# A layer-norm, linear-attention and ReLU-MLP block on one core: a new hand-written order, six normalisations moved to ScalarE, three transposes moved to DMA

## Chip, core, metric

The kernel runs on one core of one Trainium2 chip. The metric is the device time of one execution in microseconds. Lower is better.

## What is computed

The input `x` has 2048 rows of 512 bf16 values. The block is two residual branches, each behind a layer norm (mean and variance over the 512 columns, eps 1e-5, no weights):

```
ln  = layernorm(x);  q, k, v = split(ln @ wqkv)          # 32 heads of 16
phi(t) = (t + 1 if t > 0 else exp(t)) + 1e-6
kv  = sum_s phi(k)[s] (x) v[s] ;  z = sum_s phi(k)[s]    # per head
h   = x + ((phi(q) @ kv) / (phi(q) . z + 1e-6)) @ wo
out = h + relu(layernorm(h) @ w1) @ w2                   # w1: 512x1792, w2: 1792x512
```

## The kernel before

Rows are dealt to 16 tiles of 128 rows x 512 columns (`x_nat[:, t, :]`), and the tiles to four chunks of 512 rows for everything that works on transposed data (`lnT[c]`, `pqT[c]`). All of PSUM is one tensor `bk` of eight banks of 128 x 512 f32. Nothing is scheduled automatically: the string `ORDER` lists every step as a word such as `K.3.2`, and the loop at lines 548 to 550 calls `op_K(3, 2)`. The order of the words is the program order of each engine and of the DMA queue (all DMAs are issued by SyncE, one after the other), and the last number of most TensorE words is the PSUM bank. A step waits until its inputs are written and until the readers of what it overwrites are done; whatever stands behind it on the same engine waits too. So the order and the banks decide which engine idles.

The words that the change and the prediction's steps touch:

- `lx.t.n` loads n tiles of x (L201, SyncE); `lk`, `lq`, `lv`, `lo`, `l1`, `l2` load weights (L204).
- `warm.n.b`: n matmuls on zeros (L215); `const`, `masks`: small constants; `masks` is 3 memsets and 12 affine_selects on GpSimd (L181 to L193), read by `zh` and `kx`.
- First norm of tile t: `S.t`, `A.t` statistics on VectorE (L226, L227); `R.t.n` two ScalarE activations that make rstd for n tiles (L232, L233); `N.t` the normalisation itself, one VectorE tensor_scalar x - mean, times rstd, into `ln_nat` (L251).
- Transposes of a normalised tile into `lnT`: either `T.t.b`, four TensorE transposes into a bank (L270), followed by `E.t` (ScalarE, L280) or `V.t` (VectorE, L283), which copy the bank to `lnT`; or `X.t`, one DMA transpose issued by SyncE (L291). Before, tiles 0 to 6 go by T, tiles 7 to 15 by X.
- Keys: `K.t.b` four matmuls (L299); phi by `F` (exp, ScalarE, L317), `U` (relu, ScalarE, L320), `M` (min and add, VectorE, L324), `D` (add, VectorE, L327); `W` (L332) replaces U and D by one VectorE step that reads the bank. `Q.c.j.b` (L307) and `qF`, `qU`, `qM`, `qD`, `qW` are the same for queries.
- `G.t`: four matmuls that add a tile's phi(k) times `ln_nat` into banks 4 to 7 (L351); `za`, `zf`, `z`, `zc`, `zh`: the sum z.
- `gD`, `kv`, `kx` (L400), `m`, `mA` (ScalarE) or `mD` (VectorE): kv per head, masked and multiplied by wo.
- Denominators of chunk c: `dn` (L448), `dnl` and `dnx` (ScalarE, L454, L461), `dt.t` (DMA transposes, L480), `dm` (VectorE, L484). Then `h.t.b` (L494), `hD` (residual, L500), second norm `s`, `a`, `r`, `n`, transposed by `x.t` (DMA, L292) or `t.t.b` with `e` or `v`.
- MLP: `p.c.f.b` (L510), `pA` or `pD` (relu on ScalarE L516 or VectorE L521), `f` (L530), `fo` (VectorE, L538), `fd` (store, L545).

TensorE's own sequence is thus written out word by word: first the warm-up matmuls, then transposes, K and G mixed, Q, the kv product, h mixed with the first p, and p and f alternating to the end.

Of the kernel before, what the change touches and what calls it, by code (L numbers as in the profile page):

```python
# [580 lines left out]
```

## Time and profile before

| | us |
|---|---|
| median of 3 runs | 169.91 (169.8 to 170.13) |
| profiled execution, first to last instruction (span) | 168.6 |
| around the span, by the median | 1.3 |
| TensorE busy | 163.1 |
| VectorE busy | 104.7 |
| ScalarE busy | 64.3 |
| GpSimd busy | 4.8 |

A busy share is an average over stages. Matmuls are pipelined: each is shown with 379 ns though the next starts earlier, so the shown busy time hides small gaps, and gaps are found from the starts of successive groups. By stage the trace gives this (columns: window, its length, then busy us and instruction count for TensorE, its weight loads, VectorE, ScalarE, GpSimd; granted clock; DMA share; GB/s):

```profile
0.00:8.00 8.00, 5.61 (x25) 2.23 (x26) 5.27 (x19) 4.16 (x11) 4.80 (x21) 1.00 0.68 207
8.00:14.00 6.00, 5.83 (x36) 2.78 (x36) 5.62 (x17) 5.20 (x13) 0.00 (x0) 1.00 0.59 204
14.00:28.00 14.00, 14.00 (x69) 6.37 (x68) 14.00 (x37) 10.75 (x20) 0.00 (x0) 1.00 0.56 111
28.00:38.00 10.00, 10.00 (x62) 4.78 (x61) 9.53 (x16) 7.85 (x9) 0.00 (x0) 1.00 0.98 318
38.00:62.00 24.00, 23.84 (x166) 11.40 (x165) 19.80 (x39) 16.60 (x21) 0.00 (x0) 1.00 0.50 122
```

### The profile page before, as it was taken

To read this page: it belongs to the slowest core of one execution; us is meant where nothing else is said; L and a number is where in the kernel's file an instruction comes from. 1 tells how busy PE (TensorE), PEld (TensorE's weight loads), DVE (VectorE), ACT (ScalarE), POOL (GpSimd) and SP (SyncE) were. 2 spreads that over 40 slices of the span, in tenths; PEclk is the share of its full clock that TensorE was granted. 3 is DMA by queue.
4 is the path that set the end of the run, shared out by engine and by line. 5 is a ranking of instruction groups with operands and counts; after the bars stand their busy time and mean duration, and the time that the engine had idled before them with its cause. 6 is when DMAs were issued, how large, how long until landed. Compare 5 with 4: busy or idle time off the path is not lost.

```text
span 168.6 us, 2307 instructions
## 1 busy us (share of the span) xinstructions
PE 163.1 (97%) x875; PEld 76.3 (45%) x875; DVE 104.7 (62%) x207; ACT 64.3 (38%) x97; POOL 4.8 (3%) x21
## 2 busy tenths in 40 slices
...
DVE  3999999996879896978799725220066401007132
ACT  3699867775589755600201140170000203021000
POOL 7400000000000000000000000000000000000000
PEclk9999999999999999999999999999999999999999
...
GB/s 130 295 254 47 146 79 176 312 365 230 95 31 93 156 97 79 45 74 50 41 83 40 62 90 100 91 4 0 0 0 31 93 4 0 0 0 0 79 111 62
DMA packets 30091, 15.36 MB, mean 91 GB/s; under 512 B 22656, under 2 KB 29056, under 8 KB 30080
## 3 DMA queue, kind: packets, MB, share of 16 engines
...
q8 instruction: 7, 0.11, 0.3%
q14 instruction: 4, 0.03, 0.1%
HBM read 7.86 MB, written 2.10 MB: 59 GB/s over the span
## 4 chain that ended last, share of the span: by engine, by line
PE 84%; ACT 4%; DMA 4%; SPq 3%; DVE 2%; issue 1%; DVEq 0%; ACTq 0%
PE bk L530 29%; PE bk L510 29%; PE bk L351 7%; PE bk L299 7%; PE bk L494 6%; PE bk L307 5%; DMA wk_sb<-in_A_wqkv_dram 3%; ACT eb L317 1%; DMA rd<-wk_sb 1%; SPq L201 1%; SPq L480 1%; PE bk L448 1%; ACT rb L320 1%; DVE pqT L332 1%; ACT lnT L280 1%
## 5 line engine op out<-in xcount | busy, mean ns | idle before, releaser
L530 PE MATMUL bk<-w_sb,at 128*128 128x512 bf16 (+2 forms) x252 | 51.5, 355 | 0.0
L510 PE MATMUL bk<-lnT,w_sb 128*128 128x512 bf16 x224 | 51.4, 379 | 0.0
L516 ACT ACTIVATE at<-bk 128x1024 bf16<-128x1024 f32 x14 | 14.1, 1023 | 70.3 <-PE bk L510 70.3
L521 DVE TENSOR_SCALAR at<-bk 128x1024 bf16<-128x1024 f32 x14 | 17.0, 1221 | 33.7 <-PE bk L510 33.7
L530 PEld LDWEIGHTS <-at 128*128 128x128 bf16 x252 | 23.6, 98 | 25.2
L510 PEld LDWEIGHTS <-w_sb 128*128 128x128 bf16 x224 | 21.8, 98 | 26.0 <-issue 0.2
L538 DVE SCALAR_TENSOR_TENSOR gT<-bk,rstd,h_nat 128x512 bf16<-128x512 f32 (+2 forms) x18 | 12.0, 686 | 18.3 <-PE bk L530 15.9
L317 ACT ACTIVATE eb<-bk 128x1024 bf16<-128x1024 f32 (+1 forms) x18 | 16.5, 925 | 6.1 <-PE bk L299 3.5
L299 PE MATMUL bk<-wk_sb,lnT 128*128 128x512 bf16 x64 | 15.5, 379 | 0.6 <-DMA wk_sb<-in_A_wqkv_dram 0.5
L494 PE MATMUL bk<-m_sb,pqs 128*128 128x512 bf16 x64 | 15.5, 379 | 0.1
L307 PE MATMUL bk<-lnT,wq_sb 128*128 128x512 bf16 x64 | 15.1, 379 | 0.1
L320 ACT ACTIVATE rb<-bk 128x1024 bf16<-128x1024 f32 (+1 forms) x15 | 13.6, 906 | 1.2 <-PE bk L307 1.2
L351 PE MATMUL bk<-at,h_nat 128*128 128x512 bf16 x56 | 13.7, 379 | 0.0
L500 DVE TENSOR_TENSOR h_nat<-bk,x_nat 128x512 bf16<-128x512 f32 x16 | 10.8, 678 | 2.7 <-PE bk L494 2.6
L226 DVE BATCH_NORM_STATS2 st<-x_nat 128x6 f32<-128x512 bf16 x16 | 10.6, 678 | 1.8 <-DMA x_nat<-in_A_x_dram 1.8
L228 DVE BATCH_NORM_STATS2 st<-h_nat 128x6 f32<-128x512 bf16 x16 | 10.5, 679 | 0.0
L299 PEld LDWEIGHTS <-lnT 128*128 128x128 bf16 x64 | 5.9, 98 | 8.2 <-ACT lnT L280 1.2
L494 PEld LDWEIGHTS <-pqs 128*128 128x128 bf16 x64 | 6.1, 98 | 7.9 <-DVE pqs L484 1.2
L307 PEld LDWEIGHTS <-wq_sb 128*128 128x128 bf16 x64 | 6.1, 97 | 7.3 <-issue 0.4
L351 PEld LDWEIGHTS <-h_nat 128*128 128x128 bf16 x64 | 6.0, 98 | 6.6
L461 ACT ACTIVATE wk_sb<-ld 128x1024 bf16<-128x1024 f32 x8 | 8.0, 1048 | 0.1
L324 DVE TENSOR_SCALAR eb<-eb 128x1024 bf16<-128x1024 bf16 (+1 forms) x18 | 6.9, 388 | 1.2 <-ACT eb L317 1.1
...
## 6 DMA issues: line engine op xcount, KB each, us to landing
...
x_nat<-in_A_x_dram SPq DMA_DIRECT2D x2, 512.0 KB, 7.8
w_sb<-in_B_w_dram SPq DMA_DIRECT2D x2, 512.0 KB, 5.2
...
```

The lines of the kernel that those rows point to most:

```text
L299: nc.tensor.matmul(bk[:, b, :], lhsT=lnT[c][:, kd, j * P : (j + 1) * P], rhs=wk_sb[:, kd, :], start=(kd == 0), stop=(kd == KD - 1),)
L307: nc.tensor.matmul(bk[:, b, :], lhsT=wq_sb[:, kd, j * P : (j + 1) * P], rhs=lnT[c][:, kd, :], start=(kd == 0), stop=(kd == KD - 1),)
L317: nc.scalar.activation(out=buf(eb, kind, i, n), in_=bank(at_bank[kind, i], n), func=ACT.Exp)
L320: nc.scalar.activation(out=buf(rb, kind, i, n), in_=bank(at_bank[kind, i], n), func=ACT.Relu)
L351: nc.tensor.matmul(bk[:, KD + kd, :], lhsT=ln_nat[:, t, kd * P : (kd + 1) * P], rhs=pk(t)[:, 0, :], start=(t == 0), stop=(t == NT - 1),)
L494: nc.tensor.matmul(bk[:, b, :], lhsT=pqs[:, (c * KD + jb) % NQ, j * P : (j + 1) * P], rhs=m_sb[:, jb, :], start=(jb == 0), stop=(jb == KD ...
L500: nc.vector.tensor_tensor(out=h_nat[:, t : t + n, :], in0=bank(at_bank["h", t], n), in1=x_nat[:, t : t + n, :], op=ALU.add,)
L510: nc.tensor.matmul(bk[:, b, cols], lhsT=w1_sb[:, kd, f * P : (f + 1) * P], rhs=lnT[c][:, kd, cols], start=(kd == 0), stop=(kd == KD - 1),)
L516: nc.scalar.activation(out=acts[c % 2][:, f : f + n, :], in_=bank(at_bank["p", c, f], n), func=ACT.Relu)
L521: nc.vector.tensor_scalar(out=acts[c % 2][:, f : f + n, :], in0=bank(at_bank["p", c, f], n), scalar1=0.0, scalar2=None, op0=ALU.max,)
L530: nc.tensor.matmul(bk[:, b, 0 : w * P], lhsT=acts[c % 2][:, f, j * P : (j + 1) * P], rhs=w2_sb[:, f, k * P : (k + w) * P], start=(f == 0), ...
L538: nc.vector.scalar_tensor_tensor(out=o_t[:, t % NO, cols], in0=bk[:, at_bank["f", t, k], 0 : w * P], scalar=rstd2[:, t : t + 1], in1=h_nat ...
```

## The change

What is computed stays the same. All words get a new place and most TensorE words a new bank. By kind, the words differ in this:

- `N` of tiles 0, 2, 6, 9, 10, 13 is replaced by `nm.t.1` (a one-column GpSimd tensor_scalar: minus mean times rstd) and `Na.t` (ScalarE Identity activation, scale rstd, bias nm).
- `T` and `E` of tiles 3, 4, 6 are replaced by `X.3`, `X.4`, `X.6`. Of the tiles that keep T, tile 0 is now copied by V and tile 2 by E (before: the other way round), and `t.2` by `v.2` instead of `e.2`.
- `W.6.2` replaces `U.6.2` and `D.6.2`; `qU` and `qD` replace two `qW` (chunk 1 and 3, groups 2 and 3); `mD.2` replaces `mA.2`; six `pA` become `pD` and five `pD` become `pA` (13 and 15 after, 14 and 14 before).
- `masks` moves from behind lk.0 to behind `Na.13`; `const` gets two more memsets. The eleven warm-up matmuls now run in one go ahead of the first transpose.
- On SyncE: lx.0, lx.1, lx.2, lx.4.2, lx.3, lk.0, lk.2, lx.6.2, lx.8.4, X.3, X.4, lx.12.4, X.7, X.6, X.8, X.9, lv.2, lq.0, lq.2, X.12, X.13, X.10, X.11, l2.3.4 and so on. Before: lx.0, lx.2, lx.1, lx.3, lk.0, lx.4.2, lk.2, lx.6.2, lx.8.4, lx.12.4, lq.0, X.7, X.9, X.8, lq.2, X.12, ...

The diff, cut to the first part of both orders (up to the second chunk's h) and to the new steps that the order names:

```diff
 ORDER = """
-const table lx.0.1 lx.2.1 S.0 lx.1.1 S.2 A.0 S.1 A.2 R.0.1 N.0 R.2.1 lx.3.1 lk.0.2 lx.4.2 masks warm.1.7
-warm.9.7 A.1 R.1.1 T.0.6 S.3 warm.1.7 N.2 T.2.4 N.1 A.3 E.0 R.3.1 T.1.5 lk.2.2 S.4 E.1 N.3 A.4 V.2 S.5 A.5
-K.0.6 lx.6.2 K.1.3 T.3.1 F.0.1 U.0.1 lx.8.4 E.3 K.2.0 M.0.1 S.6 D.0.1 K.3.2 A.6 S.7 F.1.1 M.1.1 lx.12.4 R.4.2
-N.5 A.7 N.4 U.1.1 D.1.1 F.2.1 U.2.1 R.6.2 S.8 S.9 N.7 A.9 A.8 M.2.1 N.6 lq.0.2 G.0 T.5.1 E.5 T.4.3 G.1 X.7
-K.5.1 D.2.1 E.4 K.4.0 R.8.2 T.6.3 G.2 N.9 X.9 F.3.1 U.3.1 S.12 N.8 S.13 X.8 lq.2.2 M.3.1 A.13 A.12 D.3.1 E.6
-K.6.2 F.4.2 R.12.2 U.4.2 K.7.3 G.3 M.4.2 S.11 F.6.2 U.6.2 N.12 D.4.2 S.10 S.14 N.13 M.6.2 A.11 A.10 D.6.2 A.14
-R.10.2 X.12 K.9.1 G.4 N.11 S.15 N.10 A.15 X.13 K.8.0 G.5 G.6 za.2 U.8.2 F.8.2 X.11 X.10 G.7 R.14.2 K.13.1
-K.12.0 M.8.2 N.15 D.8.2 za.4 N.14 K.11.3 K.10.2 G.8 l2.0.3 F.12.2 U.12.2 za.6 X.15 X.14 Q.0.0.0 F.10.2 Q.0.1.1
-lv.2.2 l1.0.2 M.12.2 lv.0.2 l2.10.4 U.10.2 qU.0.0.2 qF.0.0.2 M.10.2 za.8 D.12.2 D.10.2 za.10 za.12 K.14.2 G.9
-K.15.3 F.14.2 U.14.2 G.10 Q.0.3.1 Q.0.2.0 M.14.2 qF.0.2.2 qU.0.2.2 G.11 zf.12 D.14.2 G.12 z.0.2.14 z.2.2.14
-z.1.2.14 z.3.2.14 qM.0.2.2 l2.7.3 lo.0.2 lo.2.2 l1.2.2 qM.0.0.2 qD.0.2.2 G.13 zc G.14 qD.0.0.2 zh dn.0.0 G.15
-gD.2.2 gD.0.2 Q.1.1.3 Q.1.0.2 dnl.0 dnx.0.0.2 Q.1.2.0 dnx.0.2.2 kv.3.4 kv.0.4 kv.1.4 kv.2.4 Q.1.3.1 qF.1.0.2
-qM.1.0.2 kx qF.1.2.2 qW.1.0.2 dt.0 dt.3 dt.2 dt.1 m.2.6 m.1.5 m.3.7 m.0.4 mA.0.2 Q.2.0.2 Q.2.1.3 qM.1.2.2
-mA.2.2 qW.1.2.2 dn.1.5 dm.0.0.2 dm.0.2.2 dnl.1 dnx.1.2.2 Q.2.3.1 h.3.5 hD.3 h.0.6 h.1.7 hD.0 s.3 dnx.1.0.2
-dt.6 Q.2.2.0 dt.4 dt.7 dt.5 qF.2.0.2 qU.2.0.2 h.2.6 hD.1 Q.3.0.2 Q.3.1.3 s.0 qF.2.2.2 qU.2.2.2 s.1 qU.3.0.2
-a.3 a.0 hD.2 qM.2.0.2 n.0 a.1 n.1 dm.1.0.2 dm.1.2.2 n.3 s.2 Q.3.2.0 Q.3.3.1 qD.2.0.2 a.2 qM.2.2.2 n.2 qF.3.0.2
-qF.3.2.2 l2.3.4 x.0 qM.3.2.2 qD.2.2.2 h.5.6 h.7.7 h.6.5 x.1 t.2.3 r.0.4 e.2 h.4.4 x.3 dn.2.3 dnl.2 dnx.2.0.2
-p.0.0.2 dt.8 hD.6 qM.3.0.2 qW.3.2.2 hD.4 p.0.1.3 qD.3.0.2 hD.5 dnx.2.2.2 pA.0.0.2 p.0.3.1 p.0.2.0 dn.3.6
-...
+lx.0.1 lx.1.1 const table S.0 S.1 A.0 A.1 R.1.1 lx.2.1 R.0.1 S.2 lx.4.2 nm.0.1 lx.3.1 A.2 lk.0.2 R.2.1 lk.2.2
+Na.0 N.1 S.4 warm.9.5 lx.6.2 warm.1.5 warm.1.5 nm.2.1 T.1.3 Na.2 T.0.1 E.1 S.3 T.2.6 A.3 V.0 S.5 A.4 A.5 R.3.1
+K.0.2 E.2 R.4.2 lx.8.4 N.3 N.5 U.0.1 F.0.1 N.4 K.1.5 S.6 T.5.4 X.3 M.0.1 E.5 F.1.1 K.2.0 A.6 D.0.1 S.7 U.1.1
+F.2.1 X.4 A.7 K.5.1 S.8 G.0 R.6.2 U.2.1 M.1.1 nm.6.1 K.3.2 A.8 lx.12.4 Na.6 F.3.1 N.7 S.9 D.1.1 A.9 K.4.0 M.2.1
+R.8.2 U.3.1 M.3.1 D.2.1 X.7 nm.9.1 G.1 N.8 X.6 X.8 G.2 D.3.1 Na.9 S.10 S.11 F.4.2 S.13 U.4.2 A.11 S.12 A.10 A.13
+G.3 K.7.3 A.12 R.10.2 X.9 R.12.2 M.4.2 K.6.2 F.6.2 S.15 N.12 D.4.2 nm.10.1 nm.13.1 Na.13 masks K.8.0 lv.2.2
+lq.0.2 lq.2.2 M.6.2 W.6.2 K.9.1 Na.10 X.12 G.5 F.8.2 X.13 S.14 N.11 za.2 A.14 U.8.2 G.4 M.8.2 G.6 A.15 za.4 G.7
+D.8.2 R.14.2 X.10 K.12.0 K.13.1 X.11 F.12.2 K.10.2 za.6 N.15 U.12.2 K.11.3 G.8 M.12.2 Q.0.0.0 Q.0.1.1 N.14
+U.10.2 F.10.2 qU.0.0.2 qF.0.0.2 D.12.2 za.8 M.10.2 l2.3.4 lv.0.2 X.14 Q.0.3.3 G.13 Q.0.2.2 X.15 lo.0.2 D.10.2
+K.14.0 qU.0.2.2 l2.7.3 K.15.1 G.12 za.10 qF.0.2.2 F.14.2 za.12 lo.2.2 l1.0.2 qM.0.0.2 U.14.2 G.10 G.9 G.11 zf.12
+l1.2.2 qM.0.2.2 M.14.2 D.14.2 z.1.3.14 z.0.3.14 z.2.3.14 z.3.3.14 qD.0.0.2 qD.0.2.2 G.14 zc zh dn.0.1 dnl.0
+dnx.0.2.2 G.15 gD.0.2 Q.1.1.2 Q.1.0.1 Q.1.3.4 Q.1.2.3 dnx.0.0.2 qF.1.0.2 gD.2.2 qM.1.0.2 qW.1.0.2 kv.3.5
+qF.1.2.2 kv.1.5 kv.2.5 kv.0.5 qU.1.2.2 l2.10.4 kx Q.2.0.0 m.1.2 m.3.7 m.2.6 m.0.1 dt.2 qM.1.2.2 dt.1 dt.3 dt.0
+mA.0.2 Q.2.2.4 qD.1.2.2 dn.1.3 mD.2.2 dm.0.0.2 dnl.1 dm.0.2.2 Q.2.3.5 h.3.2 h.0.7 hD.3 s.3 dnx.1.2.2 hD.0
+dnx.1.0.2 h.2.6 Q.2.1.1 hD.2 h.1.7 Q.3.3.3 qU.2.2.2 qF.2.2.2 dt.7 Q.3.2.2 s.0 s.2 dt.4 a.3 qU.2.0.2 dt.5 a.2
+qU.3.2.2 n.3 n.2 hD.1 a.0 Q.3.1.6 dt.6 qF.3.2.2 s.1 n.0 dm.1.0.2 dm.1.2.2 a.1 n.1 qF.2.0.2 x.3 t.2.7 Q.3.0.5 v.2
+qM.2.0.2 r.0.4 h.6.4 qM.2.2.2 x.0 h.7.2 h.5.0 qF.3.0.2 qU.3.0.2 hD.6 qD.2.2.2 qD.2.0.2 s.6 h.4.4 hD.5 a.6 s.5
+qM.3.0.2 x.1 l2.0.3 p.0.13.1 hD.7 dn.2.7 p.0.7.3 p.0.4.6 p.0.11.5 dnl.2 dnx.2.0.2 dnx.2.2.2 hD.4 qM.3.2.2
+p.0.5.7 p.0.12.0 dt.10 pA.0.4.2 qD.3.0.2 qD.3.2.2 pD.0.12.2 dt.11 p.0.10.4 dt.8 s.7 p.0.6.2 a.7 dt.9 dn.3.1
+p.0.2.0 dnl.3 pA.0.6.2 s.4 dnx.3.2.2 p.0.8.6 p.0.0.2 p.0.3.1 p.0.1.3 p.0.9.7 dnx.3.0.2 a.4 pA.0.2.2 dm.2.2.2 n.4
+...
 """
...
     def op_const():
...
         nc.vector.memset(ones[:], 1.0)
+        nc.vector.memset(ones32[:], 1.0)
+        nc.vector.memset(pick[:], 1.0 / Q4)
         make_identity(nc, ident[:])
...
+    def op_nm(t, n):
+        nc.gpsimd.tensor_scalar(
+            out=nmean[:, t : t + n], in0=mv[:, t : t + n, 0], scalar1=rstd[:, t : t + 1], scalar2=-1.0,
+            op0=ALU.mult, op1=ALU.mult,
+        )
+
+    def op_Na(t):
+        nc.scalar.activation(
+            out=ln_nat[:, t, :], in_=x_nat[:, t, :], func=ACT.Identity,
+            bias=nmean[:, t : t + 1], scale=rstd[:, t : t + 1],
+        )
```

The diff also defines steps that no word of the new order calls (`C`, `Nc`, `zg`, `zhi`, `zlo`, `zs`) and an empty table `HEAD` by which some tiles could be transposed ahead of their rstd; with it empty, `keys_in` is `lnT_of` and the scale of F and U is 1.0, as before.

86 lines of the change are left out of this document (63 added, 23 removed).

## Prediction

> **What bounds the kernel now.** I read the page's busy shares and slices first, then the chain that ended last, then TensorE's own timeline.
>
> ```profile
> span 168.6 us, 2307 instructions
> PE 163.1 (97%) x875; PEld 76.3 (45%) x875; DVE 104.7 (62%) x207; ACT 64.3 (38%) x97; POOL 4.8 (3%) x21
> ...
> DVE  3999999996879896978799725220066401007132
> ACT  3699867775589755600201140170000203021000
> POOL 7400000000000000000000000000000000000000
> PEclk9999999999999999999999999999999999999999
> ```
>
> TensorE is busy 97% of the span at full granted clock. VectorE is full for eight slices of 4.2 us (to about 38 us), ScalarE nearly so in slices 3 to 5, and GpSimd works in the first two slices only.
>
> ```profile
> 3.65 4.42 DMA wk_sb<-in_A_wqkv_dram
> ...
> 8.11 0.61 PE bk L299 x2
> ...
> 13.75 1.90 PE bk L299 x8
> 15.65 0.22 PE bk L270 x4
> ...
> 96.70 15.58 PE bk L510 x72
> ...
> 155.22 10.66 PE bk L530 x77
> ...
> 165.91 0.35 DVE gT L538
> ```
>
> Columns: start, length, engine and line. The second half of `wk` lands at 8.07, K.0 goes on at 8.11, and from there the end is 157.8 us of TensorE plus a tail. One 512-column matmul costs 15.58 / 72 = 0.216 us, four transposes (L270) cost 0.22. What is left to gain is (a) matmul-engine work, and (b) gaps between matmuls, which hide in the busy share, since a shown matmul overlaps the next.
>
> (b), first part, from 8.11 to 13.75: K.0's other two, K.1, K.2, K.3, G.0, G.1 are 22 x 0.216 = 4.75, T.3, T.5, T.4 are 0.66, together 5.41 in 5.64 us: 0.23 lost. Two more places:
>
> ```profile
> 44.18 1.03 PE L307 MATMUL bk<-lnT,wq_sb 128*128 128x512 bf16 x4
> 45.13 1.04 PE L404 MATMUL bk<-wo_sb,kvbd 128*128 128x512 bf16 x4
> 46.26 1.89 PE L307 MATMUL bk<-lnT,wq_sb 128*128 128x512 bf16 x8
> ...
> 53.65 3.62 PE L307 MATMUL bk<-lnT,wq_sb 128*128 128x512 bf16 x16
> 57.34 2.94 PE L494 MATMUL bk<-m_sb,pqs 128*128 128x512 bf16 x12
> 60.11 0.39 PE L270 MATMUL bk<-ident,hn 128*128 128x128 bf16 x4
> ```
>
> Starts less work: 45.13 - 44.18 - 0.86 = 0.09; 46.26 - 45.13 - 0.86 = 0.27; 57.34 - 53.65 - 3.46 = 0.23; 60.11 - 57.34 - 2.59 = 0.18. Together 0.77, with the first part **1.0 us** of gaps.
>
> **The change part by part.** *Transposes.* T.3, T.4, T.6 go: 3 x 0.22 = **0.66 us** off TensorE (875 to 863 matmuls), all behind 8.11, so on the path. T.0, T.1, T.2 lie ahead of 8.11 in both orders, where TensorE waits for `wk` anyway. The price moves to SyncE and the DMA engines:
>
> ```profile
> L291 SPq DMA_TRANSPOSE lnT<-h_nat x9: 1188/1199/1276, 14.0 to 27.4; - x9
> ...
> DMA to landing us min/median/max: 2.4/2.5/4.0
> ```
> ```profile
> 4.12 1.42 SPq L201 DMA_DIRECT2D x_nat<-in_A_x_dram  x3
> ...
> 17.99 0.57 SPq L204 DMA_DIRECT2D wq_sb<-in_A_wqkv_dram  x1
> ...
> 18.84 1.20 SPq L291 DMA_TRANSPOSE lnT<-h_nat  x1
> ```
> ```profile
> x_nat<-in_A_x_dram SPq DMA_DIRECT2D x1, 512.0 KB, 7.4
> ```
> ```profile
> 7.39 0.41 DVE L251 TENSOR_SCALAR h_nat<-x_nat,mv,rstd 128x512 bf16<-128x512 bf16 x1
> 9.82 0.60 ACT L280 ACTIVATE lnT<-bk 128x512 bf16<-128x512 bf16 x1
> 10.32 0.59 ACT L317 ACTIVATE eb<-bk 128x512 bf16<-128x512 f32 x1
> ```
>
> Each holds SyncE 1.2 us and lands 2.5 us after its start, 4.0 in the one case with a 256 KB load just ahead (18.84 behind 17.99). N.3 ran at 7.39; now two ScalarE items more (Na.0 and Na.2, less E.0, plus E.1, each 0.49 from start to start by 9.82 and 10.32) stand ahead of R.3, so N.3 ends near 8.4. X.3 starts at 8.45 and lands at 10.95, or 12.45 with a load ahead; and there is one: lx.8.4, the middle of the three at 4.12, starts at 4.6 and took 7.4, to 12.0 (with lx.12.4 and lq.0 behind it, which now go later). TensorE reaches K.3 after K.0's rest, K.1, K.2, K.5, G.0 (18 x 0.216) and T.5 (0.22): 8.11 + 4.11 = 12.2. X.4 starts near 9.7, lands at 12.2 to 13.7, and K.4 is reached at 13.1. So the wait is 0 to 0.6 us if 4.0 is the worst, and up to 1.3 if X.3 lands a full 1.5 us behind lx.8.4's 12.0. I take **0.3**: nearest the 4.0 row. lx.12.4 now stands behind X.4 on SyncE, issued near 10.9 instead of 5.1; with the 4.0 us of a queued transfer it is there at 14.9, with lx.8.4's former 7.4 at 18.3; its statistics are reached near 16 on VectorE. The queue is empty behind it now, so I take the first, which costs nothing, and keep the second for a rival. lv.2, lq.0, lq.2 (768 KB) now stand ahead of X.12 and X.13, issued near 19.2 and 20.4; with 4.0 they land at 23.2 and 24.4, when TensorE reaches K.12 and K.13 at 23.4 and 24.3: 0 to 0.5, I take 0.1.
>
> *Normalisations on ScalarE.*
>
> ```profile
> L280 ACT ACTIVATE lnT<-bk 128x512 bf16<-128x512 bf16 x6 | 3.4, 587 | 0.2 <-PE bk L270 0.2
> L461 ACT ACTIVATE wk_sb<-ld 128x1024 bf16<-128x1024 f32 x8 | 8.0, 1048 | 0.1
> L565 POOL MEMSET const-float32-0.0<- 128x1 f32 x1 | 0.1, 98 | 0.3 <-issue 0.3
> L181 POOL TENSOR_SCALAR_AFFINE_SELECT erep<-erep 32x128 bf16<-32x128 bf16 x8 | 2.4, 296 | 0.5
> ```
> ```profile
> 15.84 0.39 DVE L251 TENSOR_SCALAR h_nat<-x_nat,mv,rstd 128x512 bf16<-128x512 bf16 x1
> 16.15 0.68 DVE L226 BATCH_NORM_STATS2 st<-x_nat 128x6 f32<-128x512 bf16 x1
> ```
>
> The trace has no ScalarE activation of a 512-wide SBUF tile; its bounds are 0.52 (half of L461) and 0.59 (L280), spaced 0.49. ScalarE gains six Na and loses three E and the 1024-wide U.6 (0.92 spaced): 2.9 - 1.5 - 0.9 = +0.5 us. VectorE loses six N at 0.31 (15.84 to 16.15): -1.9, and W.6 for D.6 gives back about 0.5; so the engine that is full to 38 us is 1.4 us lighter, where it feeds every G. Each nm is a one-column GpSimd operation, between 0.1 (a memset) and 0.3 (an affine_select). nm.0 and nm.2 stand between R and Na at the very start, ahead of E.1, R.3 and all later ScalarE work; while T.0 and T.2 end before `wk` lands, up to 0.3 costs nothing, because R.2 fills ScalarE meanwhile and K.0 waits for 8.07. I take 0 and keep 0.5 us for a GpSimd operation slower than any row. The two added memsets, like the others of `const`, are 0.
>
> *Masks* go from the start of GpSimd to behind nm.13, about 19 to 24 us; `mask_h` is first read by zh, behind the last G's, so the delay itself is free.
>
> ```profile
> 4.98 0.41 DVE L251 TENSOR_SCALAR h_nat<-x_nat,mv,rstd 128x512 bf16<-128x512 bf16 x1
> ```
> ```profile
> 5.17 0.37 POOL L181 TENSOR_SCALAR_AFFINE_SELECT erep<-erep 32x128 bf16<-32x128 bf16 x1
> ...
> 5.59 0.29 POOL L181 TENSOR_SCALAR_AFFINE_SELECT erep<-erep 32x128 bf16<-32x128 bf16 x1
> ```
>
> Until now they ran beside three N. By the rows N.0 took 0.41 beside them, against 0.40 elsewhere, and one affine_select took 0.37 instead of 0.29: under 0.1 us for a meeting, mostly on GpSimd. I take **0** on TensorE's path. The Trainium skill, SBUF — State Buffer, Who interferes with whom, says that VectorE and GpSimd share a port pair that one of them holds for its whole instruction. By that rule about nine VectorE operations of that stretch would each lose up to one affine_select; the rows show a tenth of it. I weigh it as a rival.
>
> *The order.*
>
> ```profile
> 44.38 0.69 DVE kvbd L400
> 45.07 1.14 DVE pqT L332
> ```
> ```profile
> 56.59 1.29 DVE L484 TENSOR_TENSOR pqs<-pqT,rd 128x1024 bf16<-128x1024 bf16 x2 [0.46 <-DMA rd<-wk_sb]
> ```
>
> The 0.27 at 46.26 is Q.2.0 waiting for its bank, read by qW.1.0 (45.07), which stood behind kx (44.38). Now qW.1.0 stands ahead of kx, and Q.2.0 uses bank 0: that gap goes. The 0.09 of m behind kx stays. The 0.23 and 0.18 are h waiting for dm.1, which waits for the dt transposes; now h.6 comes after one Q group more (Q.3.0) and dt.7 is first, so I count 0.2 of the 0.41 back. Of the first 0.23, VectorE's relief returns 0.1; but G.1, G.2, G.5 still follow VectorE within 0.4 us by the spacings above. What is late next in the middle is dm.0.2, which VectorE now runs behind the 1024-wide mD.2, ahead of h.3: 0.1 by the same spacings. Later than 62 us VectorE and ScalarE are half idle and TensorE sees no gap over 0.1 in either order; swaps of pA for pD are 0. The tail is the same three pieces of tile 15, 0.35 us of L538 and a store: 0.
>
> **Sum**: -0.66 (transposes) - 0.27 - 0.2 - 0.1 (gaps back) + 0.3 (X.3, X.4) + 0.1 (X.12) = -0.83, and 0.1 more for dm.0.2: about **-0.75**, a span of 167.85. Around the span lie 169.91 - 168.6 = 1.3 us by the median of the runs, so **169.15 us**.
>
> **The rivals.** *Everything fits*: no wait for X.3 or X.12, and all 1.0 us of gaps go: -0.66 - 1.0 = -1.66, 168.25 us. For it: VectorE is lighter. Against: K.3's margin is under one landing's spread.
> *The early transposes are late* (slower). Place: K.3 and K.4 at 12.2 and 13.1 behind X.3 and X.4. If transposes wait for all of lx.8.4 and then need their own 1.2 us each, X.4 lands near 14.7, TensorE loses 1.6; lx.12.4, behind them on the queue, may land past 16 and move N.12 and K.12 by up to 0.7. Against -0.66 - 0.57 + 0.1 these are +0.5 with lx.12.4 in time, 170.4 us, and +1.2 with both, 171.1. It decides from the point where X.4 lands after 14.2, 1.1 us behind K.4's turn, which eats all that was gained. For it: the only transpose beside a load took 1.5 more. Against: the bytes in flight end earlier, as lx.12.4 and lq.0 are no longer behind them.
> *Masks hold VectorE*: nine operations at 0.15 to 0.3 are 1.3 to 2.7 us late between 19 and 24; W.6 has some 0.4 us before G.6, z's chain about 1. So +0.5 to +1.5 less 0.75: 169.7 to 170.7. Against: the rows above.
> *nm is slow* on GpSimd, 0.5 to 1 us: ScalarE's early work moves by as much, T.2 ends behind 8.07 and K.0 with it: 169.7 to 170.2.
>
> **How the numbers follow.** Forecast 0.54 (its own range 168.6 to 169.5), everything fits 0.10: both faster. Early transposes late 0.18, of it 0.14 slower and 0.04 the same; masks 0.11 (0.05 the same, 0.06 slower); nm 0.07 (0.04 the same, 0.03 slower). Within 0.2% (0.34 us) is about what a measurement of this kernel can't tell from no change. Faster 0.64, same 0.13, slower 0.23. The range takes in "everything fits" and the late transposes with lx.12.4 in time: 168.1 to 170.5.
>
> **What would show it.** TensorE shows 863 matmuls, L270 20 of them. K.3 and K.4 (L299, near 12.2 and 13.1) have no idle before them from a DMA over 0.3 us; landing of L291 stays at or under 4.0. The start at 8.11 is the same. No idle at Q.2.0. If GpSimd's operations between 19 and 24 stretch past 0.4, or VectorE's N and M past 0.5, the masks rival holds; if Na starts over 0.5 behind its R, nm's does. I'm wrong if the first chain piece of unbroken TensorE work starts over 0.5 later than 8.11, or gaps in 8 to 62 us add up to over 1.7.

## The result, and the profile after

| | before | after |
|---|---|---|
| median, us | 169.94 (169.80 to 170.13, 4 runs) | 174.22 (173.98 to 176.38, 4 runs) |
| profiled execution / its span | 170.13 / 168.6 | 174.24 / 172.5 |
| ratio to before, 95% interval | | 1.027 (1.022 to 1.033) |

The change makes the kernel 2.7% slower; the forecast was 0.4% faster. In some executions of the changed kernels a few microseconds run at half the granted clock, so that times of one kernel differ by up to 4.4 us; mechanisms are therefore read from starts in the trace, and a ratio with its interval.

The page of the changed kernel, the rows that answer to those of before:

```profile
span 172.5 us, 2289 instructions
PE 162.5 (94%) x847; PEld 75.4 (44%) x863; DVE 106.9 (62%) x206; ACT 64.9 (38%) x98; POOL 9.9 (6%) x27
...
POOL 1100584000000000000000000000000000000000
PEclk9999999999999999999999999999999999999999
```

TensorE's share falls from 97% to 94% with less work (863 weight loads instead of 875), at full clock. So the 3.9 us more of span are waits. The fifth to seventh digits of GpSimd (5, 8, 4) are the masks. The chain of waits shows one large piece that before had none of:

```profile
19.43 0.39 DVE h_nat L271
19.81 0.40 DVE at L370
20.21 5.82 DMA lnT<-h_nat
26.03 0.05 issue
26.08 0.39 PE bk L335
```

N.12 (L271) ends at 19.8, X.12 starts at 20.21 and lands 5.82 us later; K.12 (L335) starts 0.05 behind it. TensorE's own timeline (start, length, engine, line, tiles, count, idle before) says what that costs:

```profile
20.59 3.62 PE L394 MATMUL bk<-at,h_nat 128*128 128x512 bf16 x16
26.08 1.25 PE L335 MATMUL bk<-wk_sb,lnT 128*128 128x512 bf16 x4 [1.88 <-DMA lnT<-h_nat]
```

Sixteen matmuls by 0.216 from 20.59 end their turn at 24.04: **2.04 us lost at K.12**. SyncE's timeline around it:

```profile
9.08 2.59 SPq L328 DMA_TRANSPOSE lnT<-h_nat  x2
11.72 0.57 SPq L209 DMA_DIRECT2D x_nat<-in_A_x_dram  x1
13.35 5.12 SPq L328 DMA_TRANSPOSE lnT<-h_nat  x4
18.52 0.58 SPq L212 DMA_DIRECT2D wv_sb<-in_A_wqkv_dram  x1
19.14 0.97 SPq L212 DMA_DIRECT2D wq_sb<-in_A_wqkv_dram  x2
20.21 4.52 SPq L328 DMA_TRANSPOSE lnT<-h_nat  x3
```

SyncE stands from lx.8.4 to 9.08, because X.3 at the head of its queue waits for N.3. lx.12.4 goes out at 11.72 (before: about 5.1) and lq.0 at 19.14 (before: 5.59), 768 KB that were held back. Directly ahead of X.12 stand the three loads of 18.52 and 19.14 (lv.2, lq.0 and lq.2, 256 KB each); SyncE still issues the last of them when N.12 ends. The issue of three transposes takes 4.52 us where three cost 3.6 undisturbed. Over the kernel the landing of L328 reads so (before: 2.4/2.5/4.0):

```profile
DMA to landing us min/median/max: 2.4/2.6/5.8
```

The next loss is h.3 (L561) behind the denominators:

```profile
50.22 0.81 PE L343 MATMUL bk<-lnT,wq_sb 128*128 128x512 bf16 x3
51.84 1.43 PE L561 MATMUL bk<-m_sb,pqs 128*128 128x512 bf16 x5 [0.81 <-DVE pqs L551]
```
```profile
51.09 1.29 DVE L551 TENSOR_TENSOR pqs<-pqT,rd 128x1024 bf16<-128x1024 bf16 x2 [1.01 <-DMA rd<-wk_sb]
```

These are the last three of four matmuls (the first has its weight load but no record), so their turn ends at 50.22 + 3 x 0.216 = 50.87: 0.97 is lost, and 0.18 more inside the twelve of h. Before, this place lost nothing; the 0.23 and 0.18 that were lost at the next chunk's h are gone. VectorE itself stands 1.01 us for the dt transposes. At h.12 another 0.55 goes in the same way: two matmuls at 84.43, the next two at 85.41. Last, the end. Rows of the last pieces and of the stores on SyncE, before and then after:

```profile
159.92 6.70 SPq L545 DMA_DIRECT2D out_dram<-gT  x6
...
165.91 0.35 DVE L538 SCALAR_TENSOR_TENSOR gT<-bk,rstd,h_nat 128x128 bf16<-128x128 f32 x1 [0.30 <-PE bk L530]
```
```profile
164.23 6.06 SPq L612 DMA_DIRECT2D out_dram<-gT  x7
...
168.79 0.35 DVE L605 SCALAR_TENSOR_TENSOR gT<-bk,rstd,h_nat 128x128 bf16<-128x128 f32 x1 [0.30 <-PE bk L597]
```

VectorE's last piece ends 2.88 us later than before (169.14 against 166.26), but the last store is out 1.15 us behind it (170.29) instead of 0.36 (166.62): with the landing, the end is **1.0 us** longer.

**The ledger** of the 3.9: K.12 +2.04, the end +1.0, h.12 +0.55, h.3 +1.15, the next chunk's h -0.41, K.0's start +0.3 (all four at 7.99, where half was done before 8.11), transposes -0.66, Q.2.0 -0.27: 3.7. Steps under 0.2 us each hold the other 0.2.

### The profile page after: what moved, and what is told of

The parts are those of the page before. It is cut to its first block, busy times and chain, and to the rows that moved or that the text cites. A ratio compares the mean times of both kernels' runs of the same rounds, so it can differ in the third digit from the quotient of the medians.

```text
span 172.5 us, 2289 instructions
## 1 busy us (share of the span) xinstructions
PE 162.5 (94%) x847; PEld 75.4 (44%) x863; DVE 106.9 (62%) x206; ACT 64.9 (38%) x98; POOL 9.9 (6%) x27
## 4 chain that ended last, share of the span: by engine, by line
PE 72%; DVE 10%; DMA 8%; SPq 3%; ACT 3%; issue 2%; POOL 0%; DVEq 0%
PE bk L577 27%; PE bk L597 25%; PE bk L561 6%; PE bk L343 6%; DVE st L234 4%; PE bk L394 4%; SPq L547 3%; DMA lnT<-h_nat 3%; PE bk L335 3%; DMA rd<-wk_sb 3%; DMA x_nat<-in_A_x_dram 1%; DVE h_nat L271 1%; DVE pqs L551 1%; PE bk L515 1%; DVE st L236 1%
## 5 line engine op out<-in xcount | busy, mean ns | idle before, releaser
L597 PE MATMUL bk<-w_sb,at 128*128 128x512 bf16 (+2 forms) x249 | 50.4, 355 | 0.2
L577 PE MATMUL bk<-lnT,w_sb 128*128 128x512 bf16 x219 | 50.0, 379 | 0.3
L583 ACT ACTIVATE at<-bk 128x1024 bf16<-128x1024 f32 x13 | 13.1, 1022 | 64.0 <-PE bk L577 63.9
L588 DVE TENSOR_SCALAR at<-bk 128x1024 bf16<-128x1024 f32 x15 | 18.2, 1222 | 29.4 <-PE bk L577 29.4
L335 PE MATMUL bk<-wk_sb,lnT 128*128 128x512 bf16 x62 | 14.9, 380 | 2.1 <-DMA lnT<-h_nat 1.9
L561 PE MATMUL bk<-m_sb,pqs 128*128 128x512 bf16 x61 | 15.2, 380 | 1.3 <-DVE pqs L551 1.2
L361 ACT ACTIVATE rb<-bk 128x1024 bf16<-128x1024 f32 (+1 forms) x16 | 14.5, 912 | 4.1 <-PE bk L343 3.4
L394 PE MATMUL bk<-at,h_nat 128*128 128x512 bf16 x54 | 13.1, 379 | 0.1
L335 PEld LDWEIGHTS <-lnT 128*128 128x128 bf16 x64 | 5.9, 98 | 9.8 <-DMA lnT<-h_nat 3.0
L561 PEld LDWEIGHTS <-pqs 128*128 128x128 bf16 x64 | 5.9, 98 | 9.7 <-DVE pqs L551 3.3
```

The costliest lines, as they stand in the source:

```text
L335: nc.tensor.matmul(bk[:, b, :], lhsT=keys_in(t, kd, 1)[:, 0, :], rhs=wk_sb[:, kd, :], start=(kd == 0), stop=(kd == KD - 1),)
L361: nc.scalar.activation(out=buf(rb, kind, i, n), in_=bank(at_bank[kind, i], n), func=ACT.Relu, scale=scale_of(kind, i))
L394: nc.tensor.matmul(bk[:, KD + kd, :], lhsT=ln_nat[:, t, kd * P : (kd + 1) * P], rhs=pk(t)[:, 0, :], start=(t == 0), stop=(t == NT - 1),)
L561: nc.tensor.matmul(bk[:, b, :], lhsT=pqs[:, (c * KD + jb) % NQ, j * P : (j + 1) * P], rhs=m_sb[:, jb, :], start=(jb == 0), stop=(jb == KD ...
L577: nc.tensor.matmul(bk[:, b, cols], lhsT=w1_sb[:, kd, f * P : (f + 1) * P], rhs=lnT[c][:, kd, cols], start=(kd == 0), stop=(kd == KD - 1),)
L583: nc.scalar.activation(out=acts[c % 2][:, f : f + n, :], in_=bank(at_bank["p", c, f], n), func=ACT.Relu)
```

## The experiments

Eighteen kernels. All ratios are to the kernel before, with the 95% interval; the diffs are of the order's words.

### Is it the loads ahead of X.12?

**1. The three loads behind X.11** (changed kernel).

```diff
-K.8.0 lv.2.2 lq.0.2 lq.2.2 M.6.2 ... X.10 K.12.0 K.13.1 X.11 F.12.2
+K.8.0 M.6.2 ... X.10 K.12.0 K.13.1 X.11 lq.0.2 lq.2.2 lv.2.2 F.12.2
```

> The changed kernel with one edit: lq.0, lq.2 and lv.2 go from ahead of X.12 to behind X.11 on SyncE. Theory (the DMA transposes X.12, X.13, X.10, X.11 land late, 4.2 to 5.8 us instead of 2.5, because 768 KB of loads stand just ahead of them): the 2.0 us in which TensorE waits at K.12 go, landings of the four fall to about 2.5, the median falls from 174.2 to 172.2 (172.0 to 172.6, as Q.0.0 may wait some tenths for lq). Rival (K.12 is late because VectorE, held by the masks on GpSimd, hands out N.12 late): X.12 still starts near 20.2 and K.12 still waits over 1 us; 173.5 or more.

Measured: 1.024 (1.020 to 1.028), span 173.9. SyncE issues no load between 11.39 and 25.94, and seven transposes, X.12 at 19.70:

```profile
14.51 11.38 SPq L328 DMA_TRANSPOSE lnT<-h_nat  x7
```

TensorE's timeline:

```profile
23.98 2.96 PE L335 MATMUL bk<-wk_sb,lnT 128*128 128x512 bf16 x11
27.21 1.04 PE L335 MATMUL bk<-wk_sb,lnT 128*128 128x512 bf16 x4 [0.27 <-DMA lnT<-h_nat]
...
35.32 1.04 PE L335 MATMUL bk<-wk_sb,lnT 128*128 128x512 bf16 x4 [1.57 <-DMA lnT<-h_nat]
```

K.12 starts at 23.98 without a wait: X.12 is out 0.5 us earlier than in the changed kernel and lands after 4.2 us instead of 5.8. So the loads are worth 0.5 us of issue and 1.6 of landing there, and that ends the wait; but 2.5 was expected, and the 1.7 above it is there with no load ahead. The time stays, too: 0.6 us at the next keys, 0.3 among the queries and 1.7 at K.14, whose X.14 now stands behind five loads of 1.5 MB and lands in 6.5 us. The wait at K.12 went as the theory says, the gain didn't come: a wait was **moved**, not removed.

**2. The same three loads ahead of X.12, in the kernel before.**

```diff
-R.10.2 X.12 K.9.1
+R.10.2 lv.2.2 lq.0.2 lq.2.2 X.12 K.9.1
```

The three words leave their old places: lq.0 behind N.6, lq.2 behind X.8, lv.2 behind Q.0.1.1.

> The kernel before with one edit: lv.2, lq.0 and lq.2 go directly ahead of X.12 on SyncE, as the changed kernel has them. Theory (loads ahead of transposes alone make the wait): X.12 to X.10 land 4 to 6 us after their start, TensorE waits 1 to 2 us at K.13 or K.12, the median goes from 169.9 to 171 to 172.2. Rival (the wait needs the rest of the new order, a later N.12): 169.9 to 170.4.

Measured: 1.003 (1.000 to 1.005), span 168.7. One wait appears, and nothing else grows:

```profile
24.46 3.63 PE L299 MATMUL bk<-wk_sb,lnT 128*128 128x512 bf16 x16 [0.51 <-DMA lnT<-h_nat]
```

It is 0.67 us by starts, at K.13: the three loads hold SyncE from 17.59 to 19.78, and X.13 is out only at 21.67. X.12 lands in 4.0 us, as it does in the kernel before with 256 KB ahead, and the others in 2.5 to 2.7, where 4 to 6 was expected of all:

```profile
DMA to landing us min/median/max: 2.5/2.6/4.0
```

The start is 0.5 us earlier in return (T.3 at 8.84 instead of 9.40), presumably because the first weights land earlier without lq.0 behind them. So the theory failed here in its landings and in its size (1 to 2), and the rival's times (169.9 to 170.4) hold at their upper edge: 768 KB directly ahead of X.12 go with a landing of 5.8 and a wait of 2.0 in the changed kernel, and with 4.0 and 0.7 in the old order.

**3. Tiles 3 and 4 back on TensorE** (changed kernel, loads left).

```diff
-N.4 K.1.5 S.6 T.5.4 X.3 M.0.1 ... F.2.1 X.4 A.7
+N.4 K.1.5 S.6 T.5.4 T.3.3 V.3 M.0.1 ... K.2.0 T.4.3 ... V.4 ... F.2.1 A.7
```

> The changed kernel with only tiles 3 and 4 back on TensorE; lv.2, lq.0, lq.2 stay ahead of X.12. Theory (loads directly ahead of X.12 make the wait at K.12, whatever sent them there): lx.12.4 goes out near 5 instead of 11.7, but K.12 still waits 1.5 to 2.2 us, span 172.3 to 173.2. Rival (the early transposes themselves, through lx.12.4 and what follows from it on VectorE, make it): K.12's wait falls under 1 us, span 171.5 or less.

Measured: 1.021 (1.016 to 1.025); in the profiled execution, the longest of its runs, the key weights land late, so that all is 1.9 us later (span 175.3, above the expected 173.2).

```profile
29.67 0.61 PE L335 MATMUL bk<-wk_sb,lnT 128*128 128x512 bf16 x2 [1.58 <-DMA lnT<-h_nat]
```

K.12 still waits, 1.75 by starts, as expected: whether tiles 3 and 4 are transposed by DMA isn't what makes that wait.

### The rivals: masks, and the tail

**4. Masks back to the start** (changed kernel).

```diff
-lx.0.1 lx.1.1 const table S.0
+lx.0.1 lx.1.1 const table masks S.0
...
-nm.13.1 Na.13 masks K.8.0
+nm.13.1 Na.13 K.8.0
```

> The changed kernel with the masks moved back to the start of GpSimd. Theory (masks beside VectorE cost at most 0.1 us a meeting, mostly on GpSimd's side): 173.9 to 174.3, K.12's wait unchanged. Rival (masks hold VectorE, and with it N.12, W.6 and the z sums): 172.7 to 173.5, and VectorE's add of the z sums shrinks visibly.

Measured: 1.038 (1.033 to 1.043), span 173.7. K.12's wait is longer (2.82 by starts), not shorter, and the start gets worse: nm.0 now stands behind the masks on GpSimd, and TensorE stands 1.08 us until Na.0 lets T.0 start at 7.41. That muddles the test, so it was made again with the masks behind nm.2.

**5. Masks behind nm.2** (changed kernel).

```diff
-nm.2.1 T.1.3
+nm.2.1 masks T.1.3
```

> The changed kernel with the masks directly behind nm.2 on GpSimd (about 6 to 11 us), where GpSimd is idle until nm.6. This is the clean form of the masks question: nm is not delayed. Theory (masks beside VectorE between 19 and 28 cost TensorE nothing): span 172.2 to 172.7, median within 0.4 of the changed kernel's 174.2. Rival (masks hold VectorE): span 171.5 or less, K.12's wait shorter by over 0.5.

Measured: 1.028 (1.023 to 1.033), span 174.5. The wait at K.12 is 2.59 with no mask near it: taking the masks away from there shortens nothing. The span was expected at 172.2 to 172.7, though, and the median (175.6) within 0.4 of the changed kernel's. The rest of the span's growth is in the windows (length; busy us and counts of TensorE, weight loads, VectorE, ScalarE, GpSimd; clock; DMA share; GB/s):

```profile
24.00:27.00 3.00, 0.58 (x4) 0.11 (x2) 3.00 (x7) 0.50 (x2) 0.00 (x0) 1.00 0.91 88
27.00:31.00 4.00, 3.95 (x11) 1.46 (x11) 1.03 (x2) 0.92 (x1) 0.00 (x0) 0.57 0.76 212
```

After the wait the granted clock is 0.57 for four microseconds: 11 matmul records instead of some 19, 1.7 us more.

**6. fd.13 ahead of the last stores** (changed kernel).

```diff
-fd.14 fo.13 fd.11 fo.12 fo.15.3.1 fo.15.0.2 fd.12 fd.15.3.1 fd.13
+fd.14 fo.13 fd.11 fd.13 fo.12 fo.15.3.1 fo.15.0.2 fd.12 fd.15.3.1
```

> The changed kernel with the store fd.13 moved ahead of fd.12, right behind fd.11. Theory (the last store is issued 0.75 us after its data are ready because fd.13 and a store of 1.1 us of issue time stand in the queue ahead of it; before, it was issued at once): 173.5 to 173.7, last issue within 0.1 us of the last L605's end. Rival (the long issue belongs to the 32 KB store itself or to its data): less than 0.3 us gained, the long issue stays.

Measured: 1.023 (1.019 to 1.027), span 171.5.

```profile
164.01 5.26 SPq L612 DMA_DIRECT2D out_dram<-gT  x7
```

The seven stores are out 0.36 us behind VectorE's last piece (168.91) instead of 1.15. Of the end's 1.0, 0.8 was the order of the stores; the median (174.1, where 173.5 to 173.7 was expected) shows less of it than the trace.

### Can another order of the loads take the waits away?

**7. All loads moved** (changed kernel).

```diff
+... lx.12.4 lq.0.2 lq.2.2 ... X.15 lv.2.2 lv.0.2 ... l1.2.2 l2.10.4 ... l2.0.3 l2.3.4 l2.7.3
```

> The changed kernel with its loads placed so that none stands directly ahead of a transpose that TensorE waits for: lq.0 and lq.2 behind lx.12.4, lv, l2.10 behind X.15 with the other weights, l2.3 and l2.7 behind l2.0. Theory (loads ahead of DMA transposes are the main loss, at K.12 2.0 us, or at K.14 if they are only pushed back): no wait over 0.4 at K.12 or K.14, h.3's wait is half or less, the span falls from 172.5 to 169.8 to 170.4, the median to 171.1 to 171.8. X.7 now has 1 MB of loads ahead and may cost 0.5 at K.7. Rival (the order itself is too tight, waits only move on): span 171.5 or more.

Measured: 1.024 (1.021 to 1.026), span 173.0. No wait at K.12, but 0.60 at K.11, 0.74 at h.3, 1.06 at h.12, and 1.5 at half clock between 8 and 12 us. So the theory's span (169.8 to 170.4) is missed, and the rival's (171.5 or more) came. X.12 lands after 4.1 us here, with the last load issued 8.6 us ahead of it.

**8. The same with N.0, N.2 on VectorE and fd.13 earlier**, and **9. N.0, N.2 on VectorE alone.**

```diff
-nm.0.1 ... Na.0 N.1 ... nm.2.1 T.1.3 Na.2
+... N.1 N.0 N.2 ... T.1.3
```

> As the kernel with all loads moved, and besides: tiles 0 and 2 normalised on VectorE again, and fd.13 ahead of fd.12. Theory (the three losses add up): K.0 starts at 7.0 to 7.4 instead of 8.0, the last store is issued at once, span 168.0 to 169.0, median 169.3 to 170.3, level with the kernel before. Rival (VectorE, late by the two N, gives the start back; waits move on): 170.8 or more.

> The changed kernel with tiles 0 and 2 normalised on VectorE again (no nm.0, nm.2, Na.0, Na.2). Theory (0.27 us of nm and 0.75 us a piece of Na delay T.0 and T.2, so K.0 starts at 8.0 while wk is there near 7.1): K.0 starts at 7.0 to 7.5, but the next wait, X.12 behind loads, takes most of it back: span 171.8 to 172.4. Rival (wk sets the start, so nothing is gained): K.0 at 7.9 or later. If the gain of 0.6 or more at K.0 stays to the end, the wait at K.12 hangs on VectorE's and ScalarE's time and not only on the loads.

Measured: 1.025 (1.021 to 1.028), span 172.6, and 1.031 (1.026 to 1.036), span 171.9. Run 8 misses its theory by 3.6 us of span. In run 9, V.0 stands on VectorE behind three N and the statistics of tiles 4 and 3, and runs at 7.76:

```profile
8.21 1.04 PE L335 MATMUL bk<-wk_sb,lnT 128*128 128x512 bf16 x4 [1.32 <-DVE lnT L320]
```

So K.0 isn't earlier with N than with Na (8.21 against 7.99): the rival's number, though not its reason. In run 8, X.7 stands behind 1 MB of loads and lands in 5.2 us, and the wait turns up there (1.61 by starts):

```profile
19.01 3.63 PE L335 MATMUL bk<-wk_sb,lnT 128*128 128x512 bf16 x16 [1.45 <-DMA lnT<-h_nat]
```

**10. lx.12.4 and lq.0 early, X.3 and X.4 kept**, and **11. the same with tiles 3 and 4 on TensorE.**

```diff
-lx.8.4 N.3 ... X.3 ... X.4 A.7 ... lx.12.4 ... X.9 ... lv.2.2 lq.0.2 lq.2.2 ... l2.3.4 lv.0.2 X.14
+lx.8.4 lx.12.4 lq.0.2 N.3 ... X.3 ... X.4 A.7 ... X.9 lq.2.2 ... X.14 ... X.15 lv.2.2 lv.0.2 ... l1.2.2 l2.3.4
```

In run 11 also, as in run 3, T.3.3 V.3 and T.4.3 V.4 in place of X.3 and X.4.

> The changed kernel with the loads where the kernel before has them: lx.12.4 and lq.0 ahead of X.3, lq.2 alone ahead of X.12, lv and l2.3 behind X.15. X.3 and X.4 stay. Theory (in one queue the early loads and the early transposes exclude each other: whichever stands behind is late): K.12's wait is under 0.4, but X.3 and X.4 land 4 us or more after their start and TensorE waits 1 to 2 us at K.3; span 171.3 to 172.8. Rival (only the loads' place matters, X.3 and X.4 are harmless anywhere): K.3 waits under 0.4, span 169.8 to 170.6.

> The same loads, and tiles 3 and 4 transposed on TensorE again (T.3, T.4, copied by VectorE); X.6 stays on DMA. Theory (X.3 and X.4 are what pushed the loads back): no wait over 0.4 at K.3, K.12 or K.14, 0.44 us of transposes come back, span 169.6 to 170.6, of it about 0.7 the slow last store, 0.8 h.3. Rival (the order is too tight whatever the loads do): 171.5 or more.

Measured: 1.022 (1.018 to 1.026), span 173.0, and 1.017 (1.014 to 1.021), span 172.2. In run 10, K.12 doesn't wait, and K.3 does (1.56 by starts), and K.11 a little (0.61):

```profile
11.72 1.03 PE L394 MATMUL bk<-pk_lo,h_nat 128*128 128x512 bf16 x4
14.14 1.90 PE L335 MATMUL bk<-wk_sb,lnT 128*128 128x512 bf16 x8 [1.39 <-DMA lnT<-h_nat]
```

In run 11 neither waits over 0.4, but h.3 waits 1.16, and the span is above the theory's 169.6 to 170.6 and on the rival's side (171.5 or more). The early loads and the early transposes **exclude each other**: whichever stands first on SyncE makes the other late. That accounts for K.3 and K.12, not for all of the loss.

**12. Run 11 with fd.13 earlier, l2.3 behind l2.0 and l2.10 behind l1.2.**

```diff
-l1.2.2 l2.3.4 ... l2.10.4 kx Q.2.0.0 ... l2.0.3 p.0.13.1
+l1.2.2 l2.10.4 ... kx Q.2.0.0 ... l2.0.3 l2.3.4 p.0.13.1
```

> As the kernel with early loads and T.3, T.4, and besides fd.13 ahead of fd.12 and l2.3 behind l2.0, so that less stands ahead of the first dt. Theory (the losses are separate and add up): the last store goes out at once (0.7 less), h.3's wait under 0.4; span 168.6 to 169.6, level with the kernel before at 168.6. Rival: over 170.5.

Measured: 1.011 (1.005 to 1.016), span 169.8. h.3 starts without a wait:

```profile
49.04 1.02 PE L343 MATMUL bk<-lnT,wq_sb 128*128 128x512 bf16 x4
49.99 2.93 PE L561 MATMUL bk<-m_sb,pqs 128*128 128x512 bf16 x12
```

Of the 3.9 us lost 2.7 are back, with nothing changed but the places of loads and stores and two transposes on TensorE. The other 1.2 stay open; the expected span was 168.6 to 169.6, the rival's over 170.5, and neither came.

### What do the parts cost in the old order?

**13. Tiles 3, 4, 6 by DMA**, **14. tile 6 alone**, **15. tile 6 with X.6 behind lq.0** (kernel before).

Run 14:

```diff
-M.2.1 N.6 lq.0.2 G.0 ... T.6.3 G.2 ... E.6 K.6.2
+M.2.1 N.6 X.6 lq.0.2 G.0 ... G.2 ... K.6.2
```

Run 15 has `N.6 lq.0.2 X.6` there, and is run 14 otherwise. Run 13 is run 14 and this:

```diff
-K.1.3 T.3.1 ... lx.8.4 E.3 K.2.0 ... lx.12.4 ... N.4 U.1.1 ... T.4.3 ... E.4 K.4.0
+K.1.3 ... lx.8.4 lx.12.4 X.3 K.2.0 ... N.4 X.4 U.1.1 ... K.4.0
```

> The kernel before with one part of the change: tiles 3, 4 and 6 are transposed by DMA (X.3, X.4, X.6) instead of T and E; all loads keep their places, X.3 and X.4 stand behind lx.12.4, X.6 ahead of lq.0. Theory (a DMA transpose behind loads on the same queue lands late, and K.3 comes early): X.3 is issued near 7.8, with the 1 MB of lx.8.4 and lx.12.4 still moving, and lands at 12 to 12.5, while TensorE reaches K.3 near 10.3; a wait of 1.5 to 2.2 us there, less 0.66 of transposes: a ratio of 1.005 to 1.009 against the kernel before. Rival (a transpose lands in 2.5 us whatever moves beside it): X.3 lands at 10.4, the wait is 0.1, and the kernel is 0.5 us faster, 0.997.

> The kernel before with tile 6 alone transposed by DMA (X.6 behind N.6, ahead of lq.0). Theory: X.6 is issued near 13.5 into a nearly empty queue and lands in 2.5 us, before K.6 at about 18; TensorE saves 0.22 us and waits for nothing: 0.9987, at the edge of what can be told apart. Rival (lq.0, lq.2 and X.7 to X.13, all behind X.6 on SyncE, go 1.2 us later): a wait of 0.3 us or more at K.8, K.9 or K.12, and no gain.

> The run with tile 6 alone by DMA, with one word moved: X.6 stands behind lq.0 instead of ahead of it, so lq.0 is issued at 5.6 as in the kernel before and no load lies between X.6 and X.7. Theory (what cost 2.6 us at K.7 was one load of 256 KB held back by X.6's wait and then issued directly ahead of X.7): X.7 is issued near 16.0 and lands in 2.5 to 2.8 us, so that wait falls from 2.58 to 0.3 to 0.6; the wait of 0.95 for X.6 itself at K.6 stays, and the kernel is 0.7 to 1.4 us slower than before, 1.004 to 1.008. Rival (any transpose more on the queue ahead of X.7 does it, whatever the load): the wait at K.7 stays over 2 us and the ratio at 1.02 or above.

Measured: 1.020 (1.015 to 1.025), 1.027 (1.023 to 1.031) and 1.010 (1.007 to 1.013); spans 173.9, 173.5, 171.0. Run 13's chain:

```profile
8.15 5.81 DMA lnT<-h_nat
13.96 0.05 issue
14.01 1.48 PE bk L335 x4
```

X.3 behind 1 MB of x lands in 5.81, and K.3 loses 4.1: twice what the theory said. In run 14 one transpose, alone, costs 4.9 us: the theory of no cost is refuted, and the rival (what stands behind X.6 goes later) is right in kind and far too small. The 4.9 are waits of 0.95 and 2.58 and, behind them, 1.4 at a lower clock. TensorE, run 14 and then run 15:

```profile
17.36 1.04 PE L335 MATMUL bk<-wk_sb,lnT 128*128 128x512 bf16 x4 [0.78 <-DMA lnT<-h_nat]
20.80 1.89 PE L335 MATMUL bk<-wk_sb,lnT 128*128 128x512 bf16 x4 [2.41 <-DMA lnT<-h_nat]
```
```profile
17.93 1.04 PE L335 MATMUL bk<-wk_sb,lnT 128*128 128x512 bf16 x4 [0.76 <-DMA lnT<-h_nat]
19.23 1.04 PE L335 MATMUL bk<-wk_sb,lnT 128*128 128x512 bf16 x4 [0.26 <-DMA lnT<-h_nat]
```

The one word that differs is lq.0. Ahead of X.6 it goes out at 5.6; behind X.6, which waits for N.6, it goes out at 16.1, directly ahead of X.7, which then lands in 4.05 instead of 2.5. The second wait falls from 2.58 us (by starts) to 0.44, as expected; the first, X.6's own, stays. So the **256 KB load held back by a waiting transpose** makes it, not the transposes' number. The load alone isn't the 4.05, though: in runs 13 and 18 a transpose directly behind 256 KB lands in 3.1.

**16. All six Na in the old order**, **17. the same with the masks behind Na.10**, **18. Na of tiles 6, 9, 10, 13 with tile 6 by DMA** (kernel before).

Run 16, and what run 17 adds to it:

```diff
-N.0 ... N.2 ... N.6 ... N.9 ... N.13 ... N.10
+nm.0.1 Na.0 ... nm.2.1 Na.2 ... nm.6.1 Na.6 ... nm.9.1 Na.9 ... nm.13.1 Na.13 ... nm.10.1 Na.10
```
```diff
-lk.0.2 lx.4.2 masks warm.1.7 ... nm.10.1 Na.10 A.15
+lk.0.2 lx.4.2 warm.1.7 ... nm.10.1 Na.10 masks A.15
```

Run 18 is run 14 with nm and Na for tiles 6, 9, 10 and 13.

> The kernel before with the six normalisations of tiles 0, 2, 6, 9, 10 and 13 on ScalarE (each nm directly ahead of its Na), all else in the old order. Theory (the part costs time at the start, where tiles 0 and 2 feed the first transposes): Na.0 ends near 6.1 instead of N.0 at 5.4, T.0 moves by 0.7 and the second half of K.0, which waited for wk until 8.07, follows at 8.2 to 8.6; ScalarE's three more microseconds cost up to 0.3 more around the G's: 0.3 to 0.9 us, 1.002 to 1.005. Rival (wk alone sets the start, and VectorE's relief of 1.9 us feeds the G's sooner): no change or up to 0.3 us faster, 0.998 to 1.000.

> The run with the six normalisations on ScalarE in the old order, with the masks moved behind Na.10 on GpSimd, as the change has them behind nm.13, so that nm.2 doesn't wait for them. Theory (the masks ahead of nm.2 were 3.9 us of that run's loss; the rest is ScalarE's in-order queue, where E and U stand behind an Na that waits for its nm): the start moves by at most 0.5, K.0 at 8.1 to 8.5; waits of 1 to 2.5 us in all remain at K.4 to G's: 1.007 to 1.018. Rival (the masks were the whole loss): no more than 0.3 us over the kernel before, under 1.002.

> The kernel before with what the runs so far leave without a cost: tile 6 transposed by DMA and the normalisations of tiles 6, 9, 10 and 13 on ScalarE. Theory: 0.22 us of transposes saved, and VectorE's relief of 1.2 us and ScalarE's extra work about cancel: 169.6 to 170.0 against 169.9, 0.998 to 1.000. Rival: X.9 to X.13 start 0.4 us later each, because Na at 0.81 us ends later than N at 0.40, and K.12 waits by 0.3 us or more: 1.001 to 1.003.

Measured: 1.052 (1.049 to 1.055), 1.021 (1.018 to 1.024), 1.015 (1.012 to 1.018); spans 178.2, 173.5, 170.7. In run 16 nm.2 stands behind the masks and T.2 comes at 11.9, a fault of that experiment; run 17 takes it away, and 3.1% with it. What is left is ScalarE's queue (run 17, TensorE):

```profile
7.87 1.03 PE L305 MATMUL bk<-ident,h_nat 128*128 128x128 bf16 x8 [1.01 <-ACT h_nat L261]
```

T.2 waits for Na.2; later E.4, E.5 and E.6 stand on ScalarE behind Na.6 and Na.9, and TensorE loses 1.43 and 0.88 there and 0.62 behind a late exp. Run 18 shows the same with Na.6 alone: 1.45 us at the keys behind E.4 and E.5, and no wait over 0.6 for a DMA. All three runs are above what was expected. In the old order, then, neither part is free: the new order carries both together at 2.7%, where the transposes alone cost 2.0% and the normalisations 2.1%, 1 us or more of each at half clock in the traces of runs 13 and 17.

## Why the prediction was wrong

**The step that failed** is the last of "Transposes": "with 4.0 they land at 23.2 and 24.4 ... 0 to 0.5, I take 0.1". X.12 was issued at 20.21 instead of 19.2, landed 5.82 later instead of 4.0, and TensorE's turn came at 24.04 instead of 23.4: 1.0 + 1.8 - 0.6, less the 0.2 of slack, is the 2.04. So the term was mis-sized: 0.1 was taken, 2.04 measured. The 4.0 was one row, with 256 KB ahead; here stood 768 KB. It wasn't the only row: in the same trace X.15 (25.75) stands behind 384 KB and lands in 3.6, and x.0 (55.98) behind 512 KB in 4.3, and by runs 13 and 18 the price of 256 KB is 3.1. So the 4.0 held something else than its load, and the prediction gave it to the load. Run 1 shows that without the three loads the wait goes (0.5 of issue and 1.6 of landing less), and that 4.2 stays; run 2 that 768 KB in the old order land X.12 in 4.0 as well. The loads are thus a shown part of the 5.82, and the 1.7 of run 1 above the undisturbed 2.5 stays open; the last section says what coincides with it.

**The rival "early transposes late"** (0.18) didn't come at its place: X.3 and X.4 landed in 2.5 us and K.3 didn't wait (taken 0.3, measured 0). lx.12.4, held back behind them, landed at 16.0, and no step is seen to wait for it; in run 3 the two are gone and K.12 waits as before. What the rival had right is that loads and transposes on one queue make each other late: run 10 shows it at K.3 (1.56), run 13 too (4.1). "The queue is empty behind it now" was true at 11 us and false at 19, where the new order has put lv.2, lq.0 and lq.2 ahead of X.12.

**Terms that were right**: 0.66 for the transposes (863); Q.2.0's 0.27 is gone; nm at 0.29 within its bounds; masks at 0 on the path. (The sum itself, -0.83 and 0.1, is -0.73; the 0.02 to the -0.75 used are rounding.)

```profile
L255 POOL TENSOR_SCALAR nmean<-mv,rstd 128x1 f32<-128x1 f32 x6 | 1.7, 288 | 16.8 <-DVE st L234 6.5 <-ACT rstd L241 5.8 <-DVE h_nat L271 4.3
L189 POOL TENSOR_SCALAR_AFFINE_SELECT erep<-erep 32x128 bf16<-32x128 bf16 x8 | 5.5, 685 | 0.5
```
```profile
L261 ACT ACTIVATE h_nat<-x_nat,nmean,rstd 128x512 bf16<-128x512 bf16 x6 | 4.7, 806 | 0.0
```

**Terms that were wrong**: Na takes 0.81 us, spaced 0.72, where the bounds ended at 0.59, though a wide cast and a copy from PSUM were the nearest rows. That this cost the 0.3 at K.0's start is argued: with the two N back (run 9) K.0 came no earlier. Of "0.2 of the 0.41 back" all 0.41 came, but "0.1 for dm.0.2" at h.3 became 1.15: the prediction put the order of VectorE's steps in the sum, but the dt transposes were late on the DMA side. SyncE took 6.5 us to issue the four (before: 5.1), and the slowest landed after 4.4 us (before: 2.8), behind weight loads that went out 3 us later (32.4 to 35.6, before 28.6 to 32.9). That these loads are the cause is not shown: run 12 moves l2.3 and l2.10 and the wait is gone, but run 7 moved them too and kept 0.74. "TensorE sees no gap" past 62 us missed h.12. "The tail: 0" looked at VectorE's pieces and left out SyncE's seven stores: 1.0, of which run 6 returns 0.8.

The masks' rival is refuted by run 5, as far as K.12 goes. The Trainium skill, SBUF — State Buffer, Who interferes with whom, has whichever comes second blocked for the other's whole instruction. That the two meet, the trace confirms; but the price fell mostly on GpSimd, whose affine_selects stretch to 0.74 us from start to start (0.35 before), while VectorE's operations beside them lose 0.08 to 0.14 us each (M 0.56, in run 5 0.42). So both signs that the prediction gave for this rival, GpSimd past 0.4 and M past 0.5, came, and TensorE's path paid nothing that run 5 could give back: a sign on an engine isn't a price on the path.
